# Batch 0 by single chunks instead of pairs, with the weights requested in another order and a shorter load time in the scheduling model, in a gated linear attention and gMLP kernel

## The chip, the cores and the metric

One core of a Trainium2 chip. The metric is the device time of one execution in microseconds (us), median of several runs. A profiled execution has a span from its first to its last instruction, about 1.8 us shorter than the same run timed (169.1 against 170.86). PE is TensorE, PEld its weight loads, DVE VectorE, ACT ScalarE, POOL GpSimd, SP SyncE, which issues the loads and stores. DMA is the transfer of data between HBM (the chip's large memory) and the core; PSUM is the memory in banks that PE writes to. An eviction is the copy of a finished PSUM bank by another engine, after which PE can use the bank again. A chunk's or a load's data "land" when its last byte is reported there.

## The reference, cut to what matters

```python
B, H, S, D = 4, 8, 768, 48
for t in range(S):                                   # gated recurrence
    state = alpha[:, :, t, :, None] * state + outer(k[:, :, t], v[:, :, t])
    y[:, :, t] = q[:, :, t] @ state
x = y.transpose(0, 2, 1, 3).reshape(B, S, 384)
h = relu(x @ w_in); u, v = h[..., :512], h[..., 512:]        # w_in 384 x 1024
v_n = (v - mean(v)) / sqrt(var(v) + 1e-6)
gated = u * (w_spatial @ v_n + b_spatial)                    # w_spatial 768 x 768
out = gated @ w_out                                          # w_out 512 x 384
```

The recurrence is computed in chunks of 128 tokens: 24 chunks, six per batch, each with its alpha, k, q and v (196,608 bytes each). A batch's spatial product needs all six of its chunks. A chunk begins with ln(alpha) on ACT, then a prefix sum over it as a matmul on PE ("the chunk's prefix sum").

## The kernel before: the parts that matter

The program is not emitted in the order in which it is written. Every step is an `Op` with an estimated duration and its dependencies. A greedy scheduler, run while the program is built, picks at each step the op that can start earliest in its own model of time, and appends its instructions to their engines. On the chip each engine works through its list in order (a ready instruction behind a waiting one is shown below, with a wait of 2.08 us), and an instruction waits on semaphores for the data that it touches. The model's numbers are never seen by the chip; they decide the order alone.

```python
def schedule(ops, fill, warm_from, warm_to):
    ...
        for eng, dur in op.eng.items():
            start = max(ready, free.get(eng, 0.0))
            key = (round(start + (0.5 * dur if len(op.eng) > 1 else 0.0), 2), op.prio)
            if best is None or key < best[0]:
                best = (key, n, eng, start, dur)
    ...
        if eng == "PE":      # in the model's first 24 us: warm-up matmuls for PE's modelled idle time
            ...
            fill.append(cols)
    ...

def dma(key, us, emit, deps, prio, eng="SP", issue=0.4):
    o = op(key + ("issue",), eng, issue, emit, deps + [xfers[-8] if ... else None], prio=prio)
    x = op(key, "DMA", us, lambda _: None, [o], prio=prio, lat=2.0)     # "DMA" is an engine of the model only

# batch 0: three pairs of chunks, 384 bytes in a row in HBM (two tokens of one head)
in_=src[0, :, t0:t0 + 2 * C, :].rearrange("h (p two) d -> p h (two d)", two=2)
dma((name + "p", j), 1.52, emit, [], LOADPRIO[j][n])

# batches 1 to 3: single chunks, 192 bytes in a row
nc.sync.dma_start(out=t, in_=src[b, :, t0:t0 + C, :].rearrange("h s d -> s h d"))
dma(("ac", i), 1.08, load("ac", alpha), users("ln") + ..., P)
...
# weights: requested by POOL, which casts them to bf16 on the way
nc.gpsimd.dma_start(out=wsp_nat, in_=moe_w_spatial.rearrange("(tt p) s -> p tt s", p=128))
```

The pair form orders the tokens of 256 by even and odd, so that one contiguous run has 384 bytes; it pays with extra, half-size matmuls.

## Time and profile before

| | before |
|---|---|
| timed, median (range) | 163.69 us (163.01 to 163.70) |
| span of the profiled run | 162.1 us |
| PE busy | 146.4 us, 90% |
| DMA | full until about 117 us |

Two further stretches of the before kernel's trace are needed later (start:end, length, then busy us of PE, PEld, DVE, ACT, POOL, granted clock, DMA share, GB/s). The first runs from chunk 7's prefix sum to chunk 23's, the second from there to the last matmul:

```profile
47.30:122.30 75.00, 72.92 (x905) 47.71 (x904) 65.07 (x137) 57.60 (x143) 52.12 (x90) 1.00 0.88 187
122.30:158.50 36.20, 36.20 (x255) 21.17 (x253) 24.27 (x51) 17.47 (x43) 13.25 (x17) 1.00 0.14 50
```

PE is idle for 2.1 us of 75 in the first and not at all in the second. In this kernel no wait of ACT for an alpha appears after 50 us.

### The profile page before, as it was taken

To read this page: it belongs to the slowest core of one execution; us is meant where nothing else is said; L and a number is where in the kernel's file an instruction comes from. 1 tells how busy PE (TensorE), PEld (TensorE's weight loads), DVE (VectorE), ACT (ScalarE), POOL (GpSimd) and SP (SyncE) were. 2 spreads that over 40 slices of the span, in tenths; PEclk is the share of its full clock that TensorE was granted. 3 is DMA by queue.
4 is the path that set the end of the run, shared out by engine and by line. 5 is a ranking of instruction groups with operands and counts; after the bars stand their busy time and mean duration, and the time that the engine had idled before them with its cause. 6 is when DMAs were issued, how large, how long until landed. Compare 5 with 4: busy or idle time off the path is not lost.

```text
span 162.1 us, 4501 instructions
## 1 busy us (share of the span) xinstructions
PE 146.4 (90%) x1718; PEld 96.0 (59%) x1718; DVE 121.6 (75%) x263; ACT 100.8 (62%) x243; POOL 85.4 (53%) x151
## 2 busy tenths in 40 slices
PE   7599798089999999989999999999999999999991
PEld 6386556065765667666655666765665665556560
DVE  7848688048878999878899897777999862596830
ACT  3651782065889667666799729786899214892052
POOL 6637449001615599994644989865246367001610
PEclk9959999557999999999999999999999999999999
DMA  5999999999979898897999998989700002600025
GB/s 129 262 231 263 257 203 200 210 194 194 206 134 216 162 204 165 169 241 193 250 193 190 217 209 175 193 187 246 190 0 0 4 0 77 217 4 0 0 104 187
DMA packets 92581, 26.24 MB, mean 162 GB/s; under 512 B 87824, under 2 KB 92176, under 8 KB 92560
## 3 DMA queue, kind: packets, MB, share of 16 engines
q1 hardware_dynamic: 90816, 23.60, 66.4%
q0 software_dynamic: 1744, 2.36, 8.2%
q8 instruction: 13, 0.21, 0.5%
q14 instruction: 8, 0.07, 0.1%
HBM read 23.60 MB, written 4.72 MB: 175 GB/s over the span
## 4 chain that ended last, share of the span: by engine, by line
PE 55%; SPq 11%; DVE 10%; DMA 8%; ACT 8%; POOL 4%; issue 3%; ACTq 0%; DVEq 0%; POOLq 0%
PE ps L735 37%; SPq L905 11%; DMA vc<-in_v_dram 8%; PE pt L633 4%; PE y L342 2%; DVE ptm L674 2%; POOL gT L856 2%; DVE stats L786 2%; PE pt L663 2%; ACT cum L611 2%; PE tp L649 2%; DVE qtp L616 2%; PE cum L581 2%; PE ps L746 1%; ACT x_sb L180 1%
## 5 line engine op out<-in xcount | busy, mean ns | idle before, releaser
L856 POOL TENSOR_TENSOR gT<-vsb,uT 128x384 bf16<-128x384 f32 x28 | 25.5, 922 | 19.9 <-DVE vsb L844 19.7
L735 PE MATMUL ps<-w_spT,vn 128*128 128x384 bf16 x192 | 36.0, 326 | 0.0
L313 POOL TENSOR_TENSOR state<-state,bc 128x192 f32<-128x192 f32 x20 | 10.2, 511 | 38.5 <-ACT v_sb L186 13.4
L674 DVE TENSOR_TENSOR ptm<-pt,mask 128x512 bf16<-128x512 f32 x36 | 23.3, 683 | 2.9 <-PE pt L663 2.7
L735 PEld LDWEIGHTS <-vn 128*128 128x128 bf16 x192 | 17.3, 97 | 10.2 <-issue 0.2
L180 ACT COPY o_sb<-ps 128x384 f32<-128x384 f32 x23 | 11.0, 480 | 17.2 <-PE ps L735 17.1
L786 DVE BATCH_NORM_STATS2 stats<-v_sb 128x6 f32<-128x512 bf16 x24 | 16.4, 682 | 5.7 <-ACT v_sb L186 5.7
L735 PE MATMUL ps<-w_in_sb,xT 128*128 128x512 bf16 x72 | 19.6, 396 | 0.2 <-ACT xT L180 0.2
L844 DVE TENSOR_TENSOR vsb<-ps,bsp_bc 128x384 f32<-128x384 f32 x31 | 16.5, 554 | 3.0 <-PE ps L735 2.5
L735 PE MATMUL ps<-xT,w_in_sb 128*128 128x384 bf16 x96 | 18.3, 326 | 0.0
L605 POOL TENSOR_TENSOR ktp<-kc,binv 128x384 bf16<-128x384 f32 x18 | 16.5, 917 | 3.0 <-POOL sbd L321 1.3
L735 PE MATMUL ps<-w_out_sb,gT 128*128 128x384 bf16 x96 | 18.1, 326 | 0.0
L186 ACT ACTIVATE v_sb<-ps 128x512 bf16<-128x512 f32 x24 | 14.1, 597 | 5.4 <-PE ps L735 4.8
L180 ACT CAST x_sb<-y 128x384 bf16<-128x384 f32 x24 | 11.5, 484 | 8.0 <-PE y L691 7.5
L342 PE MATMUL y<-ident,x_sb 128*128 128x128 bf16 x72 | 8.4, 228 | 6.5 <-ACT x_sb L180 6.5
L186 ACT ACTIVATE uT<-ps 128x384 bf16<-128x384 f32 x29 | 13.0, 493 | 0.2 <-PE ps L735 0.2
L593 ACT ACTIVATE binv<-cum 128x384 bf16<-128x384 f32 x18 | 8.8, 489 | 5.9 <-PE cum L584 4.6
L735 PEld LDWEIGHTS <-gT 128*128 128x128 bf16 x96 | 8.9, 98 | 5.5
L735 PEld LDWEIGHTS <-w_in_sb 128*128 128x128 bf16 x96 | 8.5, 97 | 5.8 <-issue 0.2
L342 PEld LDWEIGHTS <-x_sb 128*128 128x128 bf16 x72 | 5.2, 100 | 9.9 <-ACT x_sb L180 7.8
L182 DVE COPY xT<-y 128x384 bf16<-128x384 bf16 x10 | 4.2, 416 | 8.8 <-PE y L342 8.7
L616 DVE TENSOR_TENSOR qtp<-qc,cum 128x384 bf16<-128x384 f32 x18 | 9.8, 547 | 0.8 <-ACT cum L611 0.8
(116 smaller groups left out, 294.8 us busy)
## 6 DMA issues: line engine op xcount, KB each, us to landing
out_dram<-o_sb SPq DMA_DIRECT2D x24, 192.0 KB, 2.1
ac<-in_alpha_dram SPq DMA_DIRECT2D x18, 192.0 KB, 4.1
kc<-in_k_dram SPq DMA_DIRECT2D x18, 192.0 KB, 3.9
qc<-in_q_dram SPq DMA_DIRECT2D x18, 192.0 KB, 3.8
vc<-in_v_dram SPq DMA_DIRECT2D x18, 192.0 KB, 3.9
ac<-in_alpha_dram SPq DMA_DIRECT2D x3, 384.0 KB, 6.1
kc<-in_k_dram SPq DMA_DIRECT2D x3, 384.0 KB, 7.2
qc<-in_q_dram SPq DMA_DIRECT2D x3, 384.0 KB, 6.6
```

The lines of the kernel that those rows point to most:

```text
L180: nc.scalar.copy(out=out, in_=in_)
L186: nc.scalar.activation(out=out, in_=in_, func=AF.Relu)
L313: nc.gpsimd.tensor_tensor(out=st["state"], in0=st["state"], in1=st["bc"][:, :, None].to_broadcast([128, HP, D]), op=ALU.mult)
L342: nc.tensor.transpose(xv[:, ks, :], st["x_sb"][:, ks, :], ident)
L605: nc.gpsimd.tensor_mul(out=kt[:, :, :, 0:D], in0=quad(st["kc"]), in1=st["binv"])
L616: nc.vector.tensor_mul(out=qt[:, :, :, 0:D], in0=quad(st["qc"]), in1=st["cv"])
L674: nc.vector.tensor_tensor(out=st["ptm"][:, s], in0=st[f"pt{s}"], in1=mask4, op=ALU.mult)
L735: return lambda ps: nc.tensor.matmul(out=out(ps), lhsT=lhsT(), rhs=rhs(), start=start, stop=stop)
L786: nc.vector.bn_stats(out=stats, in_=d["v_sb"][:, tt, :])
L844: nc.vector.tensor_tensor(out=hold["vs"], in0=ps[:, 0:TH], in1=bsp_bc[:, th, :], op=ALU.add)
L856: ENG[eng].tensor_tensor(out=bt[b]["gT"][:, dsl, cols], in0=hold["vs"], in1=bt[b]["uT"][:, dsl, cols], op=ALU.mult)
L905: nc.sync.dma_start(out=t.rearrange("p h two d -> p h (two d)"), in_=src[0, :, t0:t0 + 2 * C, :].rearrange("h (p two) d -> p h (two d)", t ...
```

## The change

Its intent: batch 0 uses the simple single-chunk form as well, so the pair form, with its extra matmuls and many constants, goes. w_in is requested as soon as the (now smaller) constants are made, w_spatial only behind the fourth chunk. With 0.8 us a load, down from 1.08, the scheduling model is told that loads are faster, and at most five may be under way in it. The diff also leaves fewer working buffers: la, kt and qt for four chunks where there was room for six, and three instead of four for kqT and ptm. Cut to its core (the buffers are left out):

```diff
+    WIN, WSP = 0, ("kc", 4)
-    IO = 3
+    IO = 6                        # single tiles instead of three pairs: the same room
+    LD, DEPTH = 0.8, 5
 ...
-        for t in ktp_bufs[:1] + qtp_bufs[:1]: ...   # constants of the pair form, four mask selects
-    def constants2(_): ...
+    def zeros(n): ...
 ...
-        o = op(key + ("issue",), eng, issue, emit, deps + [xfers[-8] if len(xfers) >= 8 ...
+        o = op(key + ("issue",), eng, issue, emit, deps + [xfers[-DEPTH] if len(xfers) >= DEPTH ...
 ...
-    def pair(j): ...                                # 150 lines: the pair form
 ...
-        dma(("ac", i), 1.08, load("ac", alpha), users("ln") + got(("lnp", (i - 2 * IO) // 2)), P)
+        dma(("ac", i), LD, load("ac", alpha), got(("ln", i - IO)), P)
 ...                                                # k, q, v likewise
+            if b == 0 and c == WIN:
+                dma(("w_in",), 5.0, w_in, got(("ac", c)), 10.0 * c, "POOL", 1.0).lat = 3.0
+            if b == 0 and c == 5:
+                dma(("w_sp",), 7.0, w_sp, got(WSP), 10.0 * c + 0.5, "POOL", 1.0).lat = 3.0
+                dma(("w_out",), 2.2, w_out, got(("vb", c)), 10.0 * c + 0.6, "POOL", 1.0).lat = 3.0
```

## The prediction

> **What bounds the kernel now.** I read the page first, for where TensorE (PE) is not full.
>
> ```profile
> span 162.1 us, 4501 instructions
> PE   7599798089999999989999999999999999999991
> PEclk9959999557999999999999999999999999999999
> DMA  5999999999979898897999998989700002600025
> ```
>
> Each digit is a slice of 4.05 us. PE has holes only in the first ten slices, with its clock halved around them. From about 40 us on it is full to the end, while DMA is full up to about 117 us. So time can be won only where PE has holes, provided that the data keep up later. The chain that ended last, in order of time, names the hole:
>
> ```profile
> 19.62 12.61 DMA vc<-in_v_dram
> 32.25 0.51 ACT vbp L180
> ...
> 131.83 26.69 PE ps L735 x157
> ```
>
> The third pair's v was requested at 19.62 and used at 32.25; the last line is the end, pure matmuls. A table of chosen stretches (start:end, length, then busy us of PE, PEld, DVE, ACT, POOL, the clock, the DMA share, GB/s) gives the sizes:
>
> ```profile
> 47.30:121.20 73.90, 71.82 (x899) 47.16 (x898) 64.00 (x133) 56.53 (x140) 51.74 (x89) 1.00 0.89 189
> 27.60:33.20 5.60, 0.08 (x3) 0.01 (x1) 0.21 (x1) 0.95 (x3) 0.84 (x2) 0.57 1.20 204
> 33.20:38.70 5.50, 5.50 (x59) 3.80 (x60) 3.31 (x8) 2.81 (x6) 0.00 (x0) 0.50 1.04 193
> ```
>
> PE did nothing for 5.6 us and then worked 5.5 us at half clock, which costs 2.75 us more: about 8.3 us. The culprit is w_spatial. The timeline shows its request at 20.29 and the queue of loads standing still behind it:
>
> ```profile
> 20.29 0.89 POOL L890 DMA_DIRECT2D wsp_nat<-in_moe_w_spatial_dram  x1
> 22.36 6.07 SPq L554 DMA_DIRECT2D kc<-in_k_dram  x1
> ...
> 32.25 0.51 ACT L180 CAST vbp<-vc 128x384 bf16<-128x384 f32 x1 [6.70 <-DMA vc<-in_v_dram]
> ```
>
> The DMA view of three stretches gives transfer speed. From 2.5 to 9 us only pair loads run (384 B in a row), from 24 to 31 us w_spatial (q0) beside the loads (q1), and in 38 to 46 us single-chunk loads alone (192 B in a row):
>
> ```profile
> DMA packets 4647, 1.76 MB, mean 271 GB/s; under 512 B 4647, under 2 KB 4647, under 8 KB 4647
> ...
> q0 software_dynamic: 732, 1.10, 87.3%
> q1 hardware_dynamic: 1012, 0.29, 25.4%
> ...
> DMA packets 8010, 1.55 MB, mean 193 GB/s; under 512 B 8007, under 2 KB 8007, under 8 KB 8007
> ```
>
> While a weight load runs, the input loads get 0.29 MB in 7 us, about a fifth of what they move alone.
>
> **What the Trainium skill says.** (1) "DMA: Bandwidth & Descriptors", section "Why small descriptors are slow (HBM only)": each small packet carries a fixed overhead. The trace agrees: 271 GB/s at 384 B, 193 GB/s at 192 B. (2) Same page, "Queues, rings and completion order": each DMA engine round-robins between queue rows at packet granularity. The packet counts fit: 732 of q0 beside 1012 of q1 over 7 us, so the queue with the far larger packets takes nearly all the time. (3) "TensorE: Matmul & The Clock Gate", "What's actually happening": an idle window of some 3.4 us throttles PE to half, a busy one releases it. The stretch at clock 0.50 after the hole agrees.
>
> **The change part by part.**
> *Single chunks in batch 0.* The 12 loads of 384 KB become 24 of 192 KB. Batch 0's 4.72 MB take 4.72/271 = 17.4 us before and, at 0.98 to 1.0 us for 192 KB (some 200 GB/s; 193 with gaps), 24 us after: DMA loses 6 to 7 us. PE gains: the pair form needs extra matmuls (prefix sums, state updates, outputs in two halves), about 1.1 us a pair by the 16 to 40 ns of such a matmul in the timeline, 3.3 us in all, but mostly where PE waited for data anyway. Counted over the program order (160 ns for a matmul of 384 columns, after rows of the chain such as 157 in 26.69 us with some wider ones among them; 213 for 512, 54 for a transpose, 25 to 50 for the small ones), PE's real work falls from 127 to 121.3 us; the count overcharges the pair form's half-size matmuls, which overlap, so I trust 3.3.
>
> *w_in first.* Its request moves from 5.77 to about 3.0 us (POOL has only two 0.3 us selects and a 0.6 us mask before it, where four mask selects of 0.7 us stood). The first w_in matmuls ran at 20.1 us; they are not the end of any wait, so this alone is worth little.
>
> *w_spatial behind chunk 4.* On POOL it now stands after the fourth chunk's k product and before the fifth's. "At most five queued" and the load time of 0.8 us exist in the kernel's own scheduling model alone: no wait on the chip holds anything back. By 1.85 us start, 1 us a load and 3.3 us lost to w_in, chunk 3's v lands near 21, its k product ends near 23.5, the request follows, and bytes flow some 3 us later (as before: request 20.29, flowing at about 23.5): from 26.5. Chunk 5's q and v should come at 27.7 and 28.7, so they are caught again: q lands near 32 and v near 35. The hole therefore shrinks but does not vanish: PE's order puts chunk 5's transposes ahead of chunks 3 and 4's outputs. I put chunk 6's prefix-sum matmul at about 41 us, with chunk 0 to 5's u and v parts done and w_spatial transposed. Before, the same state came at about 47 (chunk 7's prefix sum, 47.35, with some 2.5 us of chunk 6 already done). That is the gain: some 4 to 6 us.
>
> *What it collides with.* After chunk 6 the order of PE matters. Before, chunk 23's prefix sum comes after 91.7 of 127 us of work; after, at 79.0 of 121.3, so 42.3 us of work stand behind it, not 35.3. Before, those 35.3 took 122.28 to 158.55 = 36.3 us (factor 1.03), and 3.55 us followed (last eviction, store). After: 42.3 x 1.03 + 3.55 = 47.1 us behind chunk 23's alpha. When does that alpha land? 93 loads x 0.98 to 1.0, + 12.5 us lost to the three weights (the three stretched loads of before: 3.3, 7.4, 1.8), + 6 stores x 0.55, + 1.85 + 0.5 = 109.3 to 111.2; ln and the wait for it add 1. So the end is not before 110.3 to 112.2 + 47.1 = 157.4 to 159.3. By PE alone: 41 + 61.1 us of work up to there x 1.105 (74.9 us for 67.8 between chunks 7 and 23 before) = 108.5, + 47.1 = 155.6. DMA is thus the bound by 2 to 4 us, and gating chunk by chunk (8 and 9, 14 to 18 come late) adds about 0.5. Span: 158.5 to 160.5. The timed run adds 1.6 (163.69 against 162.1): **160.8 us**, 1.8% less.
>
> **The rivals.**
> *A. PE-bound, the gain comes whole.* 155.6 to 157 of span, 157 to 158.5 timed. For it: packets pass faster just after gaps (the start ran at 320 GB/s), stores come later, and single buffers come free earlier than pairs. Against: from 47 to 121 us DMA was already 89% busy, and single loads add 6 to 7 us.
> *B. DMA-bound with in-order engines stuck.* ACT waits for an alpha it was scheduled to have (the model's 0.8 us a load is shorter than the 0.98 to 1.0 measured), evictions stand behind it, PE starves on PSUM. Then PE holes of about 1 us per chunk appear from 50 to 110 us: 162 to 165.5 timed. For it: 24 chunks at 0.2 us x 4 are 19 us of optimism. Against: buffers for six chunks, and v, u and spatial matmuls stand between chunks.
> *C. The stall moves whole.* q of chunk 5 comes at 36 instead of 33, with a cold clock; chunk 6 at 45. Then 45 + 67.5 + 47.1 = 159.6 of span, hardly worse, since DMA hides it: about 161.
>
> **Range and chances.** The sum is most sensitive to the time of a load: 0.02 us is 1.9 us at the end. With A below and B above, 156.8 to 165. The 2% line is at 160.4, beside my number; A and half of the main case fall under it. Faster 0.46, within 2% 0.47, slower 0.07 (it needs B together with a worse start).
>
> **What would show it.** Right: a PE hole near 30 to 36 us that is shorter; wsp requested near 24; chunk 6's prefix sum near 41; alpha of chunk 23 landing at 109 to 111; DMA above 95% from 40 to 110; short PE waits on ACT's ln after chunk 8; about 47 us from chunk 23's prefix sum to the end. Wrong: chunk 23's prefix sum long after its alpha landed (PE the bound, A), DMA gaps behind stores, or a tail unlike 47 us.

## The result, and the profile after

| | before | after |
|---|---|---|
| timed, median (range) | 163.69 us (163.01 to 164.22) | 170.69 us (169.92 to 170.86) |
| ratio, 95% interval | | 1.0421 (1.037 to 1.0472): slower |
| span of the profiled run | 162.1 us | 169.1 us |

Ratios here are the mean time of one kernel's fast runs over that of the other's in the same rounds, so not quite the ratio of the medians. Executions over 1.5% slower than the fastest of the same kernel are left out of the means. The predicted 160.8 and its range up to 165.0 missed. The page of the kernel after, a slice being 4.2 us:

```profile
span 169.1 us, 4245 instructions
PE   5608898887999996868894899989999999999992
PEclk9975999999999999999999579999999999999999
DMA  5999989999799898999998999992220000610025
```

The large hole of before is gone, but PE now has gaps between 60 and 100 us, where before it was full, and a stretch at half clock (92.3 to 99.1 us). The clock is not the loss: a run of the same kernel at a mean clock of 1.0 took 169.92 us. DMA is full to 114 us. The same two stretches as before, from chunk 7's prefix sum (at 47.88 us) to chunk 23's (122.09), and from there to the last matmul:

```profile
47.90:122.10 74.20, 65.61 (x827) 43.69 (x827) 57.30 (x117) 49.15 (x125) 51.02 (x88) 0.95 0.94 195
122.10:165.70 43.60, 43.37 (x316) 25.70 (x319) 29.77 (x65) 23.95 (x59) 14.57 (x20) 1.00 0.14 51
```

Both kernels reach chunk 7 and chunk 23 within 0.6 us of each other. In between PE is idle for 8.6 us instead of 2.1 and partly cold, so it gets less done; what it did not do stands behind chunk 23, where the stretch is 43.6 us instead of 36.2. That is the 7 us.

What opens the gaps shows in ACT's and PE's timeline around chunk 18 (start, length, engine, line, operation, in brackets the idle time before and what ended it):

```profile
90.06 0.47 ACT L392 ACTIVATE cum<-cum 128x384 f32<-128x384 f32 x1
...
92.61 0.52 ACT L357 ACTIVATE la<-ac 128x384 bf16<-128x384 f32 x1 [2.08 <-DMA ac<-in_alpha_dram]
93.04 0.47 ACT L191 ACTIVATE uT<-ps 128x384 bf16<-128x384 f32 x1
...
93.56 1.12 PE L516 MATMUL ps<-w_spT,vn 128*128 128x384 bf16 x3 [2.08 <-ACT uT L191]
```

ACT's list has ln of chunk 18 next. Its alpha has not landed, so ACT waits 2.08 us. Behind it in ACT's list stands the eviction of a finished PSUM bank (uT), which needs nothing from chunk 18. (PE had written it by 89.54.) PE, in turn, waits 2.08 us for that bank, with the first spatial matmuls of the previous batch, whose data were written by 86.42. One early place in one engine's list stops two engines. The other larger gaps look alike: PE's 1.37 us before 66.57 (through a DVE product) and its 1.42 us before 74.57 end with an ACT result that stood behind a ln which had itself waited 1.55 and 1.56 us. All PE waits that the trace shows between chunk 7 and chunk 23 add up to 8.2 us, and ACT or DVE ends each of them. The list of waits between 50 and 120 us (total us, times, longest) has this at its head among those for loads:

```profile
ACT la L357 <- DMA ac<-in_alpha_dram: 12.7, 11, 2.4
POOL vb L404 <- DMA vc<-in_v_dram: 5.5, 2, 3.7
```

By chunk 23 PE is some 10 us behind: its ln runs as soon as the alpha is there, its prefix sum follows without a pause of PE before it, but only when the earlier work in PE's list is done:

```profile
111.76 0.52 ACT L357 ACTIVATE la<-ac 128x384 bf16<-128x384 f32 x1 [0.42 <-DMA ac<-in_alpha_dram]
...
122.09 0.32 PE L363 MATMUL cum<-la,ut_ones 128*128 128x384 bf16 x1
```

### The profile page after: what moved, and what is told of

Same layout as the page of the kernel before. It is cut to its first block, busy times and chain, and to the rows that moved or that the text cites. A ratio compares the mean times of both kernels' runs of the same rounds, so it can differ in the third digit from the quotient of the medians.

```text
span 169.1 us, 4245 instructions
## 1 busy us (share of the span) xinstructions
PE 144.6 (86%) x1571; PEld 97.0 (57%) x1582; DVE 115.7 (68%) x252; ACT 100.6 (60%) x244; POOL 85.9 (51%) x149
## 4 chain that ended last, share of the span: by engine, by line
PE 50%; DMA 22%; ACT 10%; DVE 6%; SPq 4%; issue 4%; POOL 2%; ACTq 0%; DVEq 0%; POOLq 0%
PE ps L516 32%; DMA ac<-in_alpha_dram 16%; DMA vc<-in_v_dram 5%; SPq L346 4%; PE pt L414 3%; PE y L177 3%; PE pt L444 3%; DVE ptm L455 2%; DMA kc<-in_k_dram 2%; PE y L324 2%; ACT la L357 2%; ACT v_sb L191 2%; PE y L472 1%; ACT x_sb L185 1%; PE ps L527 1%
## 5 line engine op out<-in xcount | busy, mean ns | idle before, releaser
L516 PE MATMUL ps<-w_spT,vn 128*128 128x384 bf16 x192 | 36.9, 334 | 2.1 <-ACT uT L191 2.1
L455 DVE TENSOR_TENSOR ptm<-pt,mask 128x512 bf16<-128x512 f32 x48 | 30.8, 680 | 5.3 <-PE pt L444 5.2
L387 POOL TENSOR_TENSOR kt<-kc,binv 128x384 bf16<-128x384 f32 x24 | 21.8, 913 | 12.9 <-issue 9.8
L357 ACT ACTIVATE la<-ac 128x384 bf16<-128x384 f32 x24 | 12.5, 522 | 20.8 <-DMA ac<-in_alpha_dram 20.7
L404 POOL CAST vb<-vc 128x384 bf16<-128x384 f32 x24 | 12.1, 503 | 17.2 <-DMA vc<-in_v_dram 10.6
L516 PE MATMUL ps<-w_in_sb,xT 128*128 128x512 bf16 x61 | 16.8, 380 | 2.3 <-ACT xT L185 1.4
L397 DVE TENSOR_TENSOR qt<-qc,cum 128x384 bf16<-128x384 f32 x24 | 13.2, 551 | 7.7 <-ACT cum L392 7.6
L516 PE MATMUL ps<-w_out_sb,gT 128*128 128x384 bf16 x96 | 18.1, 326 | 0.0
L516 PE MATMUL ps<-xT,w_in_sb 128*128 128x384 bf16 x96 | 17.9, 326 | 0.0
L185 ACT CAST x_sb<-y 128x384 bf16<-128x384 f32 x24 | 11.5, 480 | 10.5 <-PE y L472 10.4
L191 ACT ACTIVATE uT<-ps 128x384 bf16<-128x384 f32 x31 | 13.6, 489 | 0.7 <-PE ps L516 0.7
L375 ACT ACTIVATE binv<-cum 128x384 bf16<-128x384 f32 x24 | 11.6, 491 | 3.9 <-PE cum L366 2.4
L187 DVE COPY kqT<-pt 128x1024 bf16<-128x1024 bf16 x17 | 11.6, 684 | 2.8 <-PE pt L414 2.6
```

The lines of the kernel that those rows point to most:

```text
L185: nc.scalar.copy(out=out, in_=in_)
L191: nc.scalar.activation(out=out, in_=in_, func=AF.Relu)
L357: nc.scalar.activation(out=la[:, :, :, 0:D], in_=quad(st["ac"]), func=AF.Ln)
L387: nc.gpsimd.tensor_mul(out=kt[:, :, :, 0:D], in0=quad(st["kc"]), in1=st["binv"])
L397: nc.vector.tensor_mul(out=qt[:, :, :, 0:D], in0=quad(st["qc"]), in1=st["cv"])
L404: nc.gpsimd.tensor_copy(out=st["vb"], in_=st["vc"])
```

## The experiments

Theories. **1**: the order was made for loads of 0.8 us; the chip needs more (chunk 23's alpha landed at 111.7; the prediction's sum with 1.0 us a load gives 111.2), so instructions that need new data stand too early in ACT's and POOL's lists, and work that has its data waits behind them. **2**: single chunks cost DMA time in batch 0, and everything is late by that. **3**: the start, with its warm-up matmuls, costs it. **4**, formed later: any change of the model's numbers deals a new order, and this was a bad draw.

### Only the model's load time, in both kernels

```diff
-    LD, DEPTH = 0.8, 5
+    LD, DEPTH = 1.0, 5        # a_ld100; 1.2 in a_ld120
```
```diff
-        dma(("ac", i), 1.08, ...      # before, and k, q, v likewise
+        dma(("ac", i), 0.8, ...       # b_ld08
```

> The kernel after, with the load time in its scheduling model raised from 0.8 to 1.0 us; instructions, transfers and buffers are the same, only their order on the engines changes. Theory 1 (the 0.8 us order makes ACT and POOL, which work in order, wait for data that lands at 0.95 to 1.0 us a load, and PE starves behind them): about 162 us timed (160 to 165), the waits of ACT's ln for alpha fall from 20.7 us to under 8. Rival 2 (single chunks cost DMA 6 us more in batch 0 and everything is late by that): stays at 169 to 171. Rival 3 (warm-up matmuls and a late start cost it): stays at 168 to 171.

> As a_ld100, with 1.2 us. The order now puts chunk 23's prefix sum after 97.6 of 121.3 us of work instead of 79.0. Theory 1: about 160 to 163 us, ln waits for alpha under 4 us after chunk 8, alpha of chunk 23 may land later because buffers are freed later. Rivals 2 and 3: 168 to 171.

> The kernel before, with its model's time of a single-chunk load lowered from 1.08 to 0.8 us, nothing else. Theory 1: it gets slower by 2 to 5% (167 to 172 us), with ACT waiting for alpha between 50 and 110 us. Rivals 2 and 3, which lay the loss to batch 0 or to the start: unchanged within 1% (162 to 165).

a_ld100: 165.43 us, ratio to before 1.0082 (1.0036 to 1.0129). Of the 4.2% lost, 3.4 came back with the same instructions, transfers and buffers. The waits for alpha from 50 to 120 us fell from 12.7 to:

```profile
ACT la L357 <- DMA ac<-in_alpha_dram: 0.7, 1, 0.7
```

and PE is full again between chunk 7 and chunk 23, with a tail of 32 us:

```profile
52.30:128.80 76.50, 74.47 (x901) 47.86 (x905) 66.04 (x141) 58.03 (x139) 52.99 (x91) 1.00 0.86 182
128.80:161.00 32.20, 32.14 (x254) 19.14 (x252) 21.93 (x45) 16.73 (x38) 12.60 (x18) 1.00 0.16 56
```

It came to 165.43, just over the expected 160 to 165 and well over the "about 162". Its chunk 7 is reached 4.4 us later than in the kernel after (52.3 against 47.9), which fits the difference but was not tested as its cause.

b_ld08: 172.34 us, ratio 1.0477 (1.0417 to 1.0536). The kernel before, with its pairs, its w_spatial in the old place and its own start, becomes about as slow as the kernel after by one number of the model (the two intervals overlap; the expected 167 to 172 was passed by 0.3), and shows the same wait, in the same window (the profiled run, 173.84):

```profile
ACT lap L575 <- DMA ac<-in_alpha_dram: 18.1, 13, 4.0
```

This speaks strongly against theories 2 and 3 as the whole of it, for neither's cause is in this kernel. Nor are the fewer working buffers of the change, which a_ld100 keeps.

a_ld120: 169.59 to 170.68 in three runs and 163.81 in a fourth; all four missed the expected 160 to 163. Nothing waits for alpha there, but chunk 23's alpha lands at 131.7 us instead of 111.7; that this lateness is what makes it dear was not tested. Why one run was 6 us faster is not known.

### Without the warm-up matmuls

```diff
-        for cols in fill:
+        for cols in fill[:0]:     # a_nojunk: none; [:6] in a_ld100_junk6 and a_ld110_junk6
```

> The kernel after in its exact order, without its 95 warm-up matmuls (about 6 us of them stood on the chain in the first 25 us). Theory 1: within 1.5% of the kernel after (168 to 172), because an earlier start is given back in the waits for alpha from 60 us on. Rival 3 (the start costs it): 163 to 166. The clock may be low for longer at the start, which would cost a few us.

a_nojunk: 171.83 us, 1.0489 (1.0431 to 1.0546), as theory 1 expected and against theory 3. The matmuls did stand on the chain: in the chain of waits of the kernel after, two of them are

```profile
14.38 2.97 PE y L177 x18
...
18.45 1.88 PE ps L177 x23
```

but without them chunk 7 is reached at 47.3 us instead of 47.9, and the waits for alpha grow to 17.9 us.

> a_ld100 in its exact order with at most 6 warm-up matmuls at a time (they took 16 us of PE in the first 30 us there). What is left of the loss with the order mended (165.4 against 164.3) is then in the start: if warm-up matmuls stand on its chain, 161 to 163.5; if not, or if the clock falls instead, 165 to 167.

a_ld100_junk6: 164.87 us, 1.0062 (0.9991 to 1.0133), beside 1.0082 without this edit: not separable. The expected 161 to 163.5 for warm-up matmuls on the chain was not met, and no effect of them is shown.

> As a_ld100_junk6 with 1.1 us in the model, an attempt at a better version: the order that puts chunk 7 after 25.1 us of work and chunk 23 after 89.3. Theory 1: 159 to 164. If longer model times only push the loads later, over 165.

a_ld110_junk6: 168.46 us, 1.0331 (1.0232 to 1.043), a miss for theory 1 as stated (159 to 164). Nothing waits for alpha, yet PE is idle 3.4 us between 70 and 90 us, most of it behind POOL's k product and DVE's mask. This made the rival of luck worth a test of its own, below.

### The transfers made fast, the order kept

```diff
-in_=src[b, :, t0:t0 + C, :].rearrange("h s d -> s h d")
+in_=src.rearrange("b h s d -> (b h s d)").rearrange("(n p f) -> n p f", p=C, f=DM)[i].rearrange("p (h d) -> p h d", h=H)
```

The same bytes in rows of 1536 instead of 192, in the wrong places: wrong results. By the times of its packets such a load takes about 0.6 to 0.7 us (0.68 where it stands alone), where one of 192-byte rows takes 0.97 to 1.0. So it is not only as fast as the order supposes (0.8), but faster.

> The kernel after, instruction for instruction and in its own order, but each load fetches the same number of bytes as 128 rows of 1536 bytes instead of 1024 rows of 192 (the numbers land in the wrong places, so the result is wrong on purpose). It makes the transfers as fast as the order supposes, without touching the order. Theory 1 (the order supposes loads of 0.8 us, the chip needs about 0.95): 158 to 163 us timed, ACT's waits for alpha after 50 us near 0. Rival 2 (the single chunks' cost in DMA engine time) expects a gain too, but a rival 3 (start and warm-up matmuls, or the chain inside a chunk) expects 167 to 171.

> The kernel after in its own order, with the fast 1536-byte rows of a_bigrun for the six chunks of batch 0 alone (wrong result on purpose). Rival 2 (the slower single-chunk loads of batch 0 are the loss): most of the 14 us of a_bigrun come here, 158 to 162. Theory 1 (the loss is made from chunk 7 on, where the order runs ahead of the loads): an earlier start helps partly, since the loads of later chunks then also start earlier by some 10 us: 163 to 168.

> The same with the fast rows for the 18 chunks of batches 1 to 3 alone (wrong result on purpose). Theory 1: the larger part of the gain, 158 to 162, ACT's waits for alpha after 50 us gone. Rival 2: little, 166 to 170.

> Control: the kernel before in its own order (model time 1.08 us), with the fast rows for its 18 single-chunk loads (wrong result on purpose). Theory 1: its order never runs ahead of the loads, so fast loads are worth little: within 1.5% of before (161 to 164). If DMA were the bound of the kernel before as well: under 160.

a_bigrun: 156.78 us, ratio to before 0.9553 (0.9473 to 0.9632). The very order that made 170.7 us makes 156.8 when the loads come sooner than it supposes, and ACT no longer waits for any alpha after 50 us. Its page:

```profile
span 153.8 us, 4255 instructions
PE   5968888965999999999999999999999999999991
```

b_bigrun, the control: 163.29 us, 1.0043 (0.9973 to 1.0114). Faster loads in batches 1 to 3 are worth nothing to the kernel before, whose order does not run ahead of them there. Its pairs in batch 0 were left as they are, so the control matches a_bigrun_late below rather than a_bigrun. For these batches it is the order and the load time together, not DMA as such.

The two halves: fast rows in batch 0 alone 162.80 us (1.0006, 0.9925 to 1.0087), in batches 1 to 3 alone 162.91 us (160.67 to 165.33; two runs took 160.67 and 161.16). By the medians each is worth about 8 of the 14 us. For the later batches the waits for alpha are gone, as theory 1 expected; the fast runs lie in its 158 to 162, the median above. For batch 0 alone 162.80 falls between theory 2's 158 to 162 and theory 1's 163 to 168, and theory 2 has its share here: the waits remain, nearly as long as in the kernel after (12.7),

```profile
ACT la L357 <- DMA ac<-in_alpha_dram: 12.0, 10, 2.1
```

but chunk 7 is reached at 41.5 us instead of 47.9 and all that follows is earlier. Time saved on loads before a wait arrives at the end too.

### Neighbours of 0.8 and 1.0 us: load time, or luck?

> The kernel after with 0.76 us a load in its model instead of 0.8. Theory 1: 169 to 174 us, ACT's waits for alpha after 50 us over 8 us. Rival 4 (luck of the draw): anywhere from 162 to 174, not tied to those waits.

> With 0.84 us. Theory 1: 167 to 172 us, waits for alpha over 6 us. Rival 4: anywhere from 162 to 174.

> With 0.96 us. Theory 1: 163 to 167 us, waits for alpha under 4 us. Rival 4: anywhere from 162 to 174.

> With 1.04 us. Theory 1: 162 to 167 us, waits for alpha under 2 us. Rival 4: anywhere from 162 to 174.

| load time in the model, us | kernel | timed, us | ACT's waits for alpha, 50 to 120 us | chunk 23's alpha lands |
|---|---|---|---|---|
| 0.76 | a_ld076 | 172.78 to 173.43 | not read, see below | |
| 0.80 | after | 170.69 | 12.7 | 111.7 |
| 0.84 | a_ld084 | 168.12 | 7.8 | 112.4 |
| 0.96 | a_ld096 | 165.90 | 2.9 | 121.2 |
| 1.00 | a_ld100 | 165.43 | 0.7 | 122.5 |
| 1.04 | a_ld104 | 166.88 | none | 123.7 |
| 1.10 | a_ld110_junk6 | 168.46 | none | 124.0 |
| 1.20 | a_ld120 | 170.12 | none | 131.7 |
| 0.80 | b_ld08 | 172.34 | 18.1 | 107.0 |
| 1.08 | before | 163.69 | none | 112.9 |

From 0.76 to 1.00 us this is a curve and not a scatter, and the waits for alpha fall with it; its low part lies near the time that a load really takes (0.97 to 1.0). Where between 0.96 and 1.04 the lowest point is, these runs do not resolve: they are of different rounds, and the four of a_ld096 alone spread from 163.69 to 167.96. For this side theory 4 falls; for the other it stands open. The expected ranges of time were all met (a_ld104 at its upper end), those of the waits too where they could be read. In the round of the last four, one of seven runs of before took 158.15 us; medians against that round's 163.44 give 1.029, 1.015 and 1.021 for 0.84, 0.96 and 1.04, as a rough guide. The fourth run of a_ld076, the profiled one, took 205.96 us at a granted clock of 0.677; that is left out, and its trace is not used. The right side of the curve is seen but not tested: the last alpha lands later the longer the model's load time is, which would fit buffers that are freed later because chunks are consumed later.

### w_spatial alone, on the pair form

```diff
-    WIN, WSP, WOUT = ("lnp", 0), ("lnp", 2), ("qtp", 2, 1)
+    WIN, WSP, WOUT = ("lnp", 0), ("vbp", 2, 1), ("qtp", 2, 1)      # b_wsp_v
```
```diff
-                dma(("w_sp",), 3.3, w_sp, ...)
+            for n, key in enumerate((("lnp", 1), ("lnp", 2), ("vbp", 2, 1))):      # b_wsp3
+                dma(... wsp_nat[:, 2 * n:2 * n + 2] <- two of six row blocks ...)
```

> The kernel before with w_spatial requested only after the third pair's v has been used (about 27 us instead of 20.3): the part 'w_spatial later' alone, on the pair form. It should take away the PE hole at 27.6 to 33.2 us and the half clock after it. If the hole was worth its 8 us: 156 to 159. If the wait only moves to the transposes of w_spatial (landing near 39 to 40 instead of 32) and to chunk 6's loads: 161 to 165.

> An attempt at a better version: the kernel before with w_spatial in three pieces, requested behind the first pair's state, the third pair's ln and the third pair's v, so that no load of q, k or v stands behind all of it. If the hole at 27.6 to 33.2 us is the length of one weight load and can be split: 157 to 160. If each piece makes its own smaller hole or the clock stays low anyway: 161 to 164.

b_wsp_v: 163.16 us, 0.9964 (0.99 to 1.0027). Requested at 28.3 instead of 20.3, w_spatial no longer stops the third pair. Instead it stops chunk 6's q, as the chain of waits shows, and PE loses its time and clock from 40 us on:

```profile
28.34 13.14 DMA qc<-in_q_dram
```
```profile
40.00:50.00 10.00, 7.86 (x99) 6.67 (x97) 5.99 (x12) 4.99 (x10) 2.08 (x5) 0.60 1.01 199
```

The hole was moved, not removed: here too loads requested next to w_spatial pay for it.

b_wsp3, in three pieces: 161.63 us, 0.9944 (0.9881 to 1.0007). The best median of the correct versions, but its interval touches 1, so not shown to be faster than before. PE still loses 3 us from 30 to 40, and 1.3 more from 40 to 50, there at a mean clock of 0.72:

```profile
30.00:40.00 10.00, 7.01 (x103) 4.42 (x102) 7.40 (x17) 7.21 (x17) 4.20 (x8) 0.93 1.06 192
```

Two parts of the change were looked at by building the program, without a run. "At most five queued": with 8 instead of 5 in the kernel after, the built program has the same instruction order on PE, ACT, DVE and POOL, and differs only in where stores stand among the loads on SP. And "w_in first" by its key alone leaves the kernel before as it is, for there the request already follows the last constant.

## Why the prediction was wrong, point by point

- **DMA's speed and its cost in batch 0: right within half a us.** "109.3 to 111.2" for chunk 23's alpha; it landed at 111.7. DMA was full from 40 to 110 us as said (0.98 to 1.08 in each ten).
- **The tail: right.** "47.1 us behind chunk 23's alpha"; from chunk 23's prefix sum at 122.09 to the end were 47.0.
- **The step that failed** lies between these two: "ln and the wait for it add 1", "gating chunk by chunk ... adds about 0.5". ln ran at 111.76, right after the landing, but the prefix sum followed only at 122.09, because PE was behind with what stands in front of it. The 0.5 us counted the wait of a chunk for its own data. It left out that an ACT or POOL instruction waiting for a load holds up everything behind it in its list, including evictions that PE needs for other work. That term was some 10 us. The same step is wrong in "By PE alone": 67.5 us from chunk 6's prefix sum to chunk 23's at before's factor of 1.105, where 77.3 were measured. So DMA was not the bound by 2 to 4 us. The prediction's own sign "chunk 23's prefix sum long after its alpha landed" came true, but it was tied to rival A, a gain; a late PE that starves had no sign there.
- **Rival B named this mechanism** ("evictions stand behind it, PE starves on PSUM"), from the model's 0.8 against the measured 0.98, and was set aside with six chunks of buffers and other work between chunks. Buffers were no help: the loads were short (DMA at 0.98 to 1.08 from 40 to 110 us). The other work was there, but behind the waiting instruction. Its size, 162 to 165.5, was also too small.
- **The start: size off.** w_spatial was requested at 29.2, not 23.5, since POOL's fourth k product came later; so chunk 5's q and v were not caught at all (v landed at 30.1), chunk 6's were (42.9 and 44.1). Chunk 6's prefix sum came at 44.8, not 41, after waits in ACT's list in which ln of chunk 2 stood behind an eviction of v (alpha landed at 15.4, ln at 21.5), and a half clock from 10.4 to 17.2. "Some 4 to 6 us" of gain had become about 1.7 by chunk 7: the work counted by program order behind chunk 7 fell from 103.1 to 100.9 us, and it was reached 0.5 us later. That estimate rests on the counted rates, not on a run.
- **Rival A** (PE-bound, gain whole) needed loads faster than they are; with loads of 0.6 to 0.7 us (a_bigrun, 156.78) the gain does come.
- **The hole's worth.** I took 8.3 us of idle and cold PE as mostly winnable. By their medians b_wsp_v and b_wsp3 won 0.3 and 1.5 us of it by moving or splitting w_spatial, neither clear of noise.
- **The clock: half right.** The prediction's third point from the skill laid the half clock to an idle window of some 3.4 us. The records put the fall at 28.4 us, 0.8 us into the hole, so the trace does not show that the hole's length was needed.

What stays open: why with a mended order (a_ld100) nothing of the hoped gain over the kernel before is seen; why the order at 1.1 and 1.2 us loses without any wait for alpha, beyond the later loads; and why a single run of a_ld120 and of before (158.15) was much faster than its fellows.

## What to carry to other kernels

When a static order is computed from estimated transfer times, an estimate that is too short can be dear (0.8 us in the model against 0.97 to 1.0 measured cost 3.4 and 4.8% in the two kernels here): engines that keep their order wait at the early place and hold finished work behind it. Set the estimate to the time measured on the chip under load (the low part of this curve was within 5% of it), and check the list of waits for evictions that stand behind a load. The load of w_spatial took most of the DMA time while it ran (87% of 7 us); in the placements run here, moving it chose who waits, not whether.

## What the Trainium skill lacked or had wrong

- "Perfetto Trace Analysis", "Optimization Strategy": it says to find what a gap waits for and make that start sooner. Here PE's gap of 2.08 us is ended by an ACT eviction at 93.04 whose own input was ready at 89.54; the cause is one instruction ahead of it in ACT's list, waiting 2.08 us for a load. The section has no word on such waits by place in an in-order list (that the queues keep their order is told elsewhere in the skill); 12.7 us of them went with a loss of 4.2%.
- "DMA: Bandwidth & Descriptors", "Bandwidth": no figures for loads of short HBM rows from the SP queue into 128 partitions. The runs show 192 KB in 0.97 to 1.0 us at 192-byte rows (193 GB/s over a stretch), 271 GB/s at 384, and about 0.6 to 0.7 us at 1536 bytes.
- Same page, "Queues, rings and completion order": round-robin by packet is stated, not what it costs. Beside a cast load of w_spatial from POOL, the SP queue's loads got 0.29 MB in 7 us, about a fifth of their own rate.
- "TensorE: Matmul & The Clock Gate", "What's actually happening": it gives the half clock as the default and the state after at least one idle window of about 3.4 us. In the kernel after, the clock was at half from 92.3 to 99.1 us although PE's longest pause there was 2.08 us and PE was busy 1.95 of the 3.41 us before the fall; a shorter pause was enough in this trace.
